# Loading the query weights as 64-partition halves of four and a half rows, and summing five full products per bank

## The chip, the cores and the metric

The kernel runs on one core of one Trainium2 chip. The metric is the device time of one execution in microseconds (us); lower is better. The time before is the median of three runs. One further execution was recorded by the hardware profiler, and the profile views come from that one.

## The reference

Two independent problems, A and B, have the same shapes: each is one decode step of attention with a sliding window over a key/value cache. All tensors are bf16.

```python
B, Sq, D = 2, 1, 576
Hq, Hkv, Sk, Dh = 32, 16, 16384, 128
W = 4096                                   # the last 4096 cached positions
q = (x @ wq)                               # [2, 1, 4096] -> 32 heads of 128
k = k_cache[:, :, Sk - W:, :]              # each of 16 kv heads serves 2 query heads
v = v_cache[:, :, Sk - W:, :]
p = softmax(q k^T * Dh ** -0.5)
o = p v
out = o.reshape(B, Sq, Hq * Dh) @ wo       # wo: [4096, 576]
# the outputs of A and B stand side by side: [2, 1, 1152]
```

Per problem wq is 576 x 4096 elements (4.72 MB), wo 4096 x 576 (4.72 MB), and the windows of k and v are 33.6 MB each; about 153 MB in all come from HBM.

## The kernel before

**Stream and ring.** A list, `stream`, sets the order of the large loads: wq of A, wq of B, then K slabs and V slabs in turn. A slab is [128 partitions, 16384 bf16], 32 KB per partition, and holds the whole window of 4 of the 32 pairs of batch and kv head: each of a pair's 32 partitions has 128 consecutive positions. The slabs go through a ring of `NR` = 4 slots; slab n uses slot n % 4 and waits, on the SP queue, for the last reader of slab n - 4 (`reader`). All large loads are issued in order from SP's one queue. `issue_wq` places the wq loads, `issue_slab` the K and V loads, `issue_wo` the loads of wo into `wob`.

**wq before.** A contraction row of wq is 4096 columns (8192 bytes), and there are 576 = 4 x 128 + 64 rows. The first 512 rows fill one ring slot, four consecutive rows per partition (32 KB). The last 64 rows are a separate transfer into `wqr`: each row is cut in two halves of 2048 columns, so that 128 partitions hold half a row (4 KB) each. `NFC` = 4 counts the full rows per partition.

**x and q.** x of A is loaded from the ACT queue, x of B from SP's behind the loads of A's wq. The transpose `f_xT` brings x to 128 partitions with five small matmuls against an identity: four for the full rows and one for a copy (`x_dup`) of the last 64 elements with each element doubled. ACT copies the result into `xT` (`f_xev`, L389); DVE multiplies the doubled part with a mask (`maskP`) of even and odd partitions (`f_xev2`, L397), so that each half row of `wqr` meets only its own x element. `do_qpair` (matmuls recorded at L450 and, for those that keep the weights, at L188) computes q for two groups of heads at a time into four PSUM banks of 512 columns: a bank sums four products from the ring slot and one from `wqr`. There are four such pairs, two per problem, 20 products of 512 columns each. `do_qrow` moves a finished q row to SBUF (ACT), transposes it in 32x32 blocks (DVE, L475) and keeps it in `qk` (ACT, L483); `do_zq` (POOL) spreads it into the zero-padded weights of the score product.

**Attention.** For each of 16 steps a K slab is transposed in four quarters by DVE into `xt` (`do_X`, L515; three buffers), multiplied with `zq` on PE into the score banks `ST` (`do_S`, L540), reduced and exponentiated (`do_max`, `do_nm`, `do_exp`), transposed back (`do_pC`), and multiplied with the V slab (`do_PV`, L631). The output projection (`do_proj`) follows per group with wo in `wob`.

**Memory shared over time.** `wob` holds 32 slots of wo; its second half is used early on, before wo arrives, for `wqr`, `qrow`, `qtr`, `xT`, `x_sb` and the identity (`early`). wo's first load waits for the last `qkeep`.

**Order.** Each engine runs its instructions in the order in which `S.add` recorded them, and waits on semaphores for what another engine or a DMA produces. All q pairs and q rows stand ahead of the first `do_X` on every engine.

Of the kernel before, what the change touches and what calls it, by code (L numbers as in the profile page):

```python
# [5 lines left out]
FP32 = mybir.dt.float32  # L6
# [53 lines left out]
def build_kernel(nc, probs, out, cfg=None):  # L60
# [24 lines left out]
    GPP = SPP // 2  # L85
    NFC = D // 128
    DREM = D - 128 * NFC
    assert DREM * 2 == 128 and NFC * HD == SLABW
    HH = HD // 2
    NXC = NFC + 2  # L90
    NOUT = wo0.shape[1]
# [22 lines left out]
    with es:  # L114
        sb = lambda name, shape, dt: es.enter_context(nc.sbuf_tensor(name, shape, dt))
        ring = sb("ring", [128, NR, SLABW], BF16)
        xt = sb("xt", [128, NKT, 2048], FP32)
        wob = sb("wob", [128, NSW, NOUT], BF16)
        used = [0]

        def early(shape):
            n = 1
            for d_ in shape:
                n *= d_
            a = wob[:, NSW // 2:NSW, :].rearrange("p s n -> p (s n)")[:, used[0]:used[0] + n]
            used[0] += n
            assert used[0] <= NSW // 2 * NOUT
            names = "abc"[:len(shape)]
            return a if len(shape) == 1 else a.rearrange("p (%s) -> p %s" % (" ".join(names), " ".join(names)), **dict(zip(names, shape)))
        wqr = early([NPROB, HH])  # L130
        qrow = early([1024])
        qtr = early([1024])
        xT = early([NXC, NPROB, 128])
        x_sb = early([D])[0:NPROB * Bb]
        x_dup = early([DREM, 2])[0:NPROB * Bb]
        ident_b = early([128])
# [18 lines left out]
        Rsb = [sb("Rsb%d" % n_, [128, Bb, n], BF16) for n_, n in enumerate((32, 16))]  # L155
        masks = sb("masks", [128, 30], BF16)
        maskS, mask16D, maskA, mask4S, maskJ, maskP = (masks[:, a_:b_] for a_, b_ in ((0, 8), (8, 16), (16, 20), (20, 24), (24, 28), (28, 30)))
        mask16S = sb("mask16S", [128, 16], BF16)
# [19 lines left out]
        ring_sem = [sem("ring%d" % r) for r in range(NR)]  # L178
        wq_sem = sem("wq")
        wo_sem = [sem("wo%d" % r) for r in range(2)]  # L180
# [21 lines left out]
        def load_x(P, eng):  # L202
# [5 lines left out]
        p_ident_b = S.add("pool", lambda e: e.affine_select(ident_b[:], ones_b[:], [[-1, 128]], ALU.is_equal, 0.0,  # L208
                                                           base=0, channel_multiplier=1), [p_ones_b], "ident_b")
        p_zxT = S.add("dve", lambda e: e.memset(xT[:].rearrange("c h p w -> c (h p w)").bitcast(FP32), 0.0), [], "zero_xT")  # L210
        p_zq = S.add("dve", lambda e: e.memset(zq[:].rearrange("d p z w -> d (p z w)").bitcast(FP32), 0.0), [], "zero_zq")
# [14 lines left out]
        for part, at in ((0, ("K", 5)), (1, ("V", 11)), (2, ("V", 12))):  # L226
            w_at.setdefault(at, []).append(part)

        slab_dma = {}
        pieces = []  # L230
# [8 lines left out]
        def issue_slab(n):  # L239
# [6 lines left out]
            src = src_t.rearrange("b h s d -> (b h) s d")[g::SPP, Sk - W:Sk, :].rearrange("c (r j) d -> r c (j d)", r=32)  # L246
            r = n % NR
            deps = [reader[n - NR]] if n >= NR else []
# [10 lines left out]
        def issue_wq(n, P):  # L259
            wqP = probs[P][3]  # L260
            r = n % NR
            deps = [reader[n - NR]] if n >= NR else []
            wq_dma[P] = dma_op("sp", wq_sem, 1, lambda e: e.dma_start(
                wqr[:, P, :], wqP[NFC * 128:D, :].rearrange("r (h n) -> r h n", h=2)).then_inc(wq_sem, 16), [], "wqr%d" % P)
            slab_dma[n] = dma_op("sp", ring_sem[r], 1, lambda e: e.dma_start(
                ring[:, r, :], wqP[0:NFC * 128, :].rearrange("(p s) n -> p (s n)", s=NFC)).then_inc(ring_sem[r], 16), deps, "wq%d" % P)

            if P == 0:
                for P_ in range(1, NPROB):
                    x_dma[P_] = load_x(P_, "sp")  # L270
# [96 lines left out]
        def f_xT(e, bank):  # L367
            last = None
            NB = NPROB * Bb
            for ch in range(NFC + 1):  # L370
                if ch < NFC:
                    src = x_sb[0:NB, 0:NFC * 128].rearrange("b (p s) -> b s p", s=NFC)[:, ch, :]
                else:
                    src = x_dup[0:NB, :, :].rearrange("b r t -> b (r t)")
                last = e.matmul(bank[:, ch * 4 * NB:(ch + 1) * 4 * NB], src, ident_b[0:NB, 0:NB].rearrange(  # L375
                    "k (p b) -> k p b", b=Bb).unsqueeze(2).broadcast_to([NB, NPROB, 4, Bb]), start=True, stop=True)
            return last
        issue_until(0)
        init_small()
        x_cd = S.add("dve", lambda e: e.tensor_copy(  # L380
            x_dup[:], x_sb[:, NFC * 128:D].unsqueeze(2).broadcast_to([NPROB * Bb, DREM, 2])), list(x_dma.values()), "xdup")
        init["maskP"] = S.add("dve", lambda e: e.tensor_reduce(
            maskP[:], ident_b[:].rearrange("d (r t) -> d t r", t=2), AX.X, ALU.max), [p_ident_b], "maskP")

        n_x, bank_x, op_xT = tb_job(f_xT, "xT", list(x_dma.values()) + [x_cd, p_ident_b])

        def f_xev(e):
            NB = NPROB * NFC * 4
            return e.activation(  # L389
                xT[:, 0:NFC].rearrange("c h p (a w) -> c (h p a) w", a=4)[:, :, 0:Bb],  # L390
                bank_x[:, 0:NB * Bb].rearrange("c (q b) -> c q b", b=Bb),
                ACTF.Copy)
        op_xev = S.add("act", f_xev, [op_xT, p_zxT], "xev")
        NB_ = NPROB * 4 * Bb

        def f_xev2(e):
            return e.tensor_tensor(  # L397
                xT[:, NFC:NXC].rearrange("c h p (a w) -> c h (p a) w", a=4)[:, :, :, 0:Bb],
                bank_x[:, NFC * NB_:(NFC + 1) * NB_].rearrange("c (q b) -> c q b", b=Bb).unsqueeze(1).broadcast_to([128, 2, NPROB * 4, Bb]),
                maskP[:].unsqueeze(2).unsqueeze(3).broadcast_to([128, 2, NPROB * 4, Bb]), ALU.mult)  # L400
        op_xev = S.add("dve", f_xev2, [op_xev, op_xT, init["maskP"]], "xev2")
        tb_consumer[n_x] = op_xev

# [20 lines left out]
        def do_qpair(i):  # L424
# [4 lines left out]
            banks = q_banks(i)  # L429
            mine = lambda ch: [b for b in range(4) if ch < NFC or b % 2 == ch - NFC]  # L430
            order = [NFC, NFC + 1] + list(range(NFC))
            if Gs[0] % GPP:
                order = order[::-1]
            todo_ = [(ch, b) for ch in order for b in mine(ch)]
            seen = {b: 0 for b in range(4)}
# [3 lines left out]
            for g in range(2):  # L439
                def fn(e, part=todo_[(0, ends[0])[g]:ends[g]]):  # L440
                    last = None
                    for ch, b in part:
                        c0 = (b % 2) * HH + 512 * (Gs[b // 2] % GPP)
                        w_ = ring[:, nq % NR, ch * HD + c0:ch * HD + c0 + 512] if ch < NFC else wqr[:, P, c0 - (b % 2) * HH:c0 - (b % 2) * HH + 512]
                        start, stop = seen[b] == 0, seen[b] == NFC
                        seen[b] += 1
                        if q_first[0] == (P, ch):
                            last = matmul_again(e, q_first[1], banks[b], w_, start, stop, False)
                        else:
                            last = q_first[1] = e.matmul(banks[b], xT[:, ch, P, :], w_, start=start, stop=stop)  # L450
                            q_first[0] = (P, ch)
                    return last
                before = [q_free.get((i - 1, b)) for b in range(4)] if g else []
                op = S.add("pe", fn, [slab_dma[nq], op_xev] + list(wq_dma.values()) + prev + before, "q%d" % Gs[g])
                reader[nq] = op
# [52 lines left out]
        def do_X(s, u):  # L508
# [3 lines left out]
            deps = [slab_dma[n]]  # L512
            if i >= NKT:
                deps.append(Sop[divmod(i - NKT, NU)])
            Xop[(s, u)] = S.add("dve", lambda e: e.transpose(  # L515
                xt[:, i % NKT, :].rearrange("k (j w) -> k j w", w=64),
                ring[:, n % NR, :].bitcast(FP32).rearrange("k (j q w) -> k q j w", q=4, w=64)[:, u]),
                deps, "X%d_%d" % (s, u))
# [99 lines left out]
        def do_PV(D_, rounds, wait):  # L618
# [7 lines left out]
            def f(e):  # L626
                last = None
                for jr in rounds:
                    for cb in range(4):
                        j0_ = JR * jr + 4 * cb  # L630
                        last = e.matmul(ACC[32 * cb:32 * cb + 32, 0:512],  # L631
                                        pC[:, D_ % NPT, j0_:j0_ + 4, :].rearrange("k j c -> k (j c)"),
                                        ring[:, n % NR, j0_ * 128:(j0_ + 4) * 128],
                                        start=(jr == 0), stop=(jr == last_r))
# [389 lines left out]
```

## Time and profile before

| quantity | value |
|---|---|
| median of 3 runs | 363.33 us (362.79 to 363.37) |
| the profiled execution | 363.02 us |
| its span in the profile | 361.8 us |
| mean granted TensorE clock | 0.882 |
| PE busy | 218.6 us (60%) |
| DVE busy | 200.9 us (56%) |
| ACT busy | 68.2 us (19%) |
| POOL busy | 35.3 us (10%) |
| read from HBM | 153.10 MB, 423 GB/s over the span |

The profiled execution is one execution; its span runs from the first to the last instruction, and 1.2 us of its time lie outside. A DMA's "time to landing" counts from its issue, so it includes the time for which the transfer stands in the queue behind others. A DMA share is the mean busy share of the core's 16 DMA engines.

### The profile page before, as it was taken

To read this page: it belongs to the slowest core of one execution; us is meant where nothing else is said; L and a number is where in the kernel's file an instruction comes from. 1 tells how busy PE (TensorE), PEld (TensorE's weight loads), DVE (VectorE), ACT (ScalarE), POOL (GpSimd) and SP (SyncE) were. 2 spreads that over 40 slices of the span, in tenths; PEclk is the share of its full clock that TensorE was granted. 3 is DMA by queue.
4 is the path that set the end of the run, shared out by engine and by line. 5 is a ranking of instruction groups with operands and counts; after the bars stand their busy time and mean duration, and the time that the engine had idled before them with its cause. 6 is when DMAs were issued, how large, how long until landed. Compare 5 with 4: busy or idle time off the path is not lost.

```text
span 361.8 us, 2730 instructions
## 1 busy us (share of the span) xinstructions
PE 218.6 (60%) x1318; PEld 55.8 (15%) x945; DVE 200.9 (56%) x175; ACT 68.2 (19%) x149; POOL 35.3 (10%) x55
## 2 busy tenths in 40 slices
PE   0399195763747207466574737766867707657786
PEld 0010021120111101112120201212121201211132
DVE  4112599846647019283756658392919239079931
ACT  1036502130203002103020203020201203002131
POOL 1000000004000400001300040002100040200020
PEclk9999689997889857969698978899898978969999
DMA  8999999999999999999999999999999999999996
GB/s 348 421 449 406 464 406 437 431 408 453 415 442 438 428 424 438 429 428 438 417 446 422 435 428 442 426 435 428 424 424 440 431 424 433 431 438 428 438 409 248
DMA packets 6491, 153.27 MB, mean 424 GB/s; under 512 B 712, under 2 KB 1232, under 8 KB 1616
## 3 DMA queue, kind: packets, MB, share of 16 engines
q1 hardware_dynamic: 6476, 153.10, 98.8%
q8 instruction: 9, 0.15, 0.2%
q14 instruction: 2, 0.02, 0.0%
q10 hardware_dynamic: 4, 0.00, 0.0%
HBM read 153.10 MB, written 0.00 MB: 423 GB/s over the span
## 4 chain that ended last, share of the span: by engine, by line
DMA 72%; DVE 17%; PE 7%; ACT 3%; SPq 1%; issue 0%
DMA ring<-in_B_k_cache_dram 34%; DMA ring<-in_A_k_cache_dram 27%; DVE xt L515 14%; DMA wob<-in_B_wo_dram 8%; DMA wob<-in_B_x_dram 3%; PE st L188 3%; PE st L540 3%; ACT wob L465 1%; DVE wob L475 1%; ACT qk L483 1%; PE st L450 1%; DVE m L550 1%; ACT wob L470 1%; DVE nM L563 0%; SPq L252 0%
## 5 line engine op out<-in xcount | busy, mean ns | idle before, releaser
L515 DVE STREAM_TRANSPOSE xt<-ring 128x2048 f32<-128x2048 f32 x64 | 145.3, 2284 | 86.6 <-DMA ring<-in_A_k_cache_dram 49.8
L540 PE MATMUL st<-xt,zq 128*128 128x512 bf16 x256 | 111.6, 436 | 122.6 <-DVE xt L515 98.1
L188 PE MATMUL st<-xt,zq 128*128 128x512 bf16 x256 | 110.1, 430 | 0.0
L540 PEld LDWEIGHTS st<-xt,zq 128*128 128x128 bf16 x256 | 27.1, 106 | 216.3 <-DVE xt L515 113.5
L631 PE MATMUL acc<-ring,pC 128*32 128x512 bf16 x512 | 32.5, 381 | 1.2 <-DMA ring<-in_B_v_cache_dram 1.2
L568 ACT ACTIVATE nMrep<-nM 1x128 f32<-1x128 f32 x16 | 4.9, 308 | 146.9 <-DVE nM L563 146.9
L643 ACT ACTIVATE acc_sb<-acc 128x512 bf16<-128x512 f32 x16 | 9.5, 596 | 79.9 <-PE acc L631 79.9
L593 DVE STREAM_TRANSPOSE pC<-pR 128x1024 bf16<-128x1024 bf16 x16 | 19.6, 1223 | 3.7 <-ACT pR L585 2.1
L650 POOL TENSOR_TENSOR acc_sb<-acc_sb,masks 128x1024 bf16<-128x1024 bf16 (+1 forms) x8 | 13.4, 1679 | 66.6 <-ACT acc_sb L643 66.6
L550 DVE TENSOR_REDUCE m<-st 128x1 f32<-128x1024 f32 x16 | 19.0, 1190 | 1.4 <-PE st L188 1.4
L502 POOL TENSOR_TENSOR zq<-qk,masks 128x128 bf16<-128x128 bf16 x16 | 6.3, 398 | 136.2 <-PE st L188 114.4
L585 ACT ACTIVATE pR<-st,bias_sb 128x1024 bf16<-128x1024 f32 x16 | 17.8, 1114 | 0.5
L475 DVE STREAM_TRANSPOSE wob<-wob 128x512 f32<-128x512 f32 x8 | 5.7, 711 | 20.3 <-ACT wob L465 12.9
L415 ACT ACTIVATE st<-maskB 128x1024 f32<-128x1024 bf16 x16 | 16.5, 1032 | 1.6 <-POOL rsel L600 0.4
L786 PE MATMUL ot<-wob,Rsb 128*2 128x512 bf16 x56 | 15.2, 390 | 0.0
L631 PEld LDWEIGHTS acc<-ring,pC 128*32 128x32 bf16 x512 | 12.4, 96 | 15.9 <-issue 3.2
L600 POOL TENSOR_TENSOR rsel<-masks,rsum 128x16 f32<-128x16 bf16 x8 | 1.7, 216 | 108.0 <-ACT pR L585 108.0
L188 PE MATMUL tb<-wob,Rsb 128*2 128x64 bf16 x56 | 10.9, 195 | 0.0
L375 PE MATMUL tb<-wob 4*128 4x16 bf16 x5 | 0.3, 179 | 14.5 <-DVE wob L380 14.5
L653 POOL TENSOR_TENSOR acc_sb<-acc_sb 128x512 bf16<-128x512 bf16 (+1 forms) x8 | 8.2, 1029 | 0.6
L188 PE MATMUL st<-ring,wob 128*128 128x512 bf16 x24 | 7.9, 445 | 0.0
L579 ACT ACTIVATE bias_sb<-tb 128x1 f32<-128x1 f32 x16 | 2.7, 171 | 24.8 <-PE tb L573 24.8
(89 smaller groups left out, 99.5 us busy)
## 6 DMA issues: line engine op xcount, KB each, us to landing
ring<-in_A_k_cache_dram SPq DMA_DIRECT2D x8, 4096.0 KB, 30.4
ring<-in_A_v_cache_dram SPq DMA_DIRECT2D x8, 4096.0 KB, 32.5
ring<-in_B_k_cache_dram SPq DMA_DIRECT2D x8, 4096.0 KB, 28.4
ring<-in_B_v_cache_dram SPq DMA_DIRECT2D x7, 4096.0 KB, 32.8
wob<-in_A_wo_dram SPq DMA_DIRECT2D x1, 4608.0 KB, 43.3
ring<-in_A_wq_dram SPq DMA_DIRECT2D x1, 4096.0 KB, 12.7
ring<-in_B_wq_dram SPq DMA_DIRECT2D x1, 4096.0 KB, 22.6
ring<-in_B_v_cache_dram SPq DMA_DIRECT2D x1, 3072.0 KB, 25.5
```

Source lines behind the costliest of these rows:

```text
L188: return e.add_instruction(mybir.InstMatmult(name=nc.get_next_instruction_name(), engine=i.engine, ins=[e.lower_ap(rhs), i.ins[1]], outs=[ ...
L415: chain[(s, "fill")] = S.add("act", lambda e: e.activation(ST[s % 2][:, :].rearrange("k (h j) -> k h j", h=2), maskB[:].unsqueeze(1).broad ...
L475: chain[(G, "qtr")] = S.add("dve", lambda e: e.transpose(qtr[:].bitcast(FP32), qrow[:].bitcast(FP32)), evs, "qtr%d" % G)
L515: Xop[(s, u)] = S.add("dve", lambda e: e.transpose(xt[:, i % NKT, :].rearrange("k (j w) -> k j w", w=64), ring[:, n % NR, :].bitcast(FP32) ...
L540: first = last = e.matmul(bank, zq[:, p4, s % NZQ, w0:w0 + 128], mv, start=False, stop=stop, skip_group_check=True)
L550: chain[(s, "max")] = S.add("dve", lambda e: e.tensor_reduce(m1[:, 0:1], ST[s % 2][:, :], AX.X, ALU.max), d, "max%d" % s)
L585: chain[(s, "exp")] = S.add("act", lambda e: e.activation(pR[:, :], ST[s % 2][:, :], ACTF.Exp, bias=bias_sb[:, 0:1], scale=SCALE, accum_ou ...
L593: chain[(s, "pC")] = S.add("dve", lambda e: e.transpose(pC[:, s % NPT, :, :].rearrange("k j c -> k (j c)"), pR[:, :]), d, "pC%d" % s)
L631: last = e.matmul(ACC[32 * cb:32 * cb + 32, 0:512], pC[:, D_ % NPT, j0_:j0_ + 4, :].rearrange("k j c -> k (j c)"), ring[:, n % NR, j0_ * 1 ...
L643: acc_ev[D_] = S.add("act", lambda e: e.activation(acc_sb[:, D_ % 2, :], ACC[:, :], ACTF.Copy), d, "accev%d" % D_)
L650: t = S.add("pool", lambda e: e.tensor_tensor(v, v, maskJ[:].unsqueeze(1).unsqueeze(3).broadcast_to([128, l1 - l0, 4, 128]), ALU.mult), [a ...
L786: first = e.matmul(OT[0:Bb, 0:NB0], l_, wob[:, w0 + s_, 0:NB0], start=start and begin, stop=end, skip_group_check=True)
```

## The change

All 576 rows of wq now come in one form. A problem's wq, read as one string of bytes, is cut into 128 pieces of 36,864 bytes, which is four and a half rows. Even pieces go to partitions 0 to 63 and odd pieces to partitions 64 to 127. An odd piece begins in the middle of a row, so it is written half a row (`HH` = 2048 columns) further on in its partition; this brings column c of every row to the same place in all partitions. Each half is one DMA of [64 partitions, 18432 bf16]; both stand on SP's queue where the two loads of wq stood.

A partition now spans five rows (`NFC` = 5, 40,960 bytes), of which half a row is filled with zeros by DVE (`f_zw`, four memsets): the last half row on partitions 0 to 63, the first on 64 to 127. Because this is 8192 bytes more than a ring slot, `ring`, `xt` and `wob` become parts of one tensor `big`: A's wq ends with slot 0 and starts in the last `xt` buffer, B's wq fills slot 3 and runs into the start of `wob`. The slots are used in the order 0, 3, 1, 2. The third X transpose, the first to write that `xt` buffer, waits for the last product that reads A's wq.

x is gathered by two ACT copies into `x_s`, five columns for the even and five for the odd partitions; five small matmuls transpose them, and one ACT copy fills `xT`. `x_dup`, `maskP`, `f_xev2` and `wqr` go. Each bank of q sums five products of 512 columns with all 128 partitions; there are 20 products per pair, as before.

```diff
-    NFC = D // 128
+    NFC = D // 128 + 1
...
+        big = sb("big", [128, WOB0 + NSW * NOUT], BF16)
+        xt = big[:, 0:RING0].bitcast(FP32).rearrange("k (n w) -> k n w", n=NKT)
+        ring = big[:, RING0:WOB0].rearrange("k (n w) -> k n w", n=NR)
+        wob = big[:, WOB0:WOB0 + NSW * NOUT].rearrange("k (s n) -> k s n", n=NOUT)
+        wq_at = [RING0 - EXT, WOB0 - SLABW]
...
+        def f_zw(e):
+            last = None
+            for a_ in wq_at:
+                for e_ in range(2):
+                    z0 = a_ + (1 - e_) * (NFC * HD - HH)
+                    last = e.memset(big[64 * e_:64 * e_ + 64, z0:z0 + HH].bitcast(FP32), 0.0)
+            return last
+        p_zw = S.add("dve", f_zw, [], "zero_w")
...
+        slot = [(0, 3, 1, 2)[n % NR] for n in range(len(stream))]
...
-            wq_dma[P] = dma_op("sp", wq_sem, 1, lambda e: e.dma_start(
-                wqr[:, P, :], wqP[NFC * 128:D, :].rearrange("r (h n) -> r h n", h=2)).then_inc(wq_sem, 16), [], "wqr%d" % P)
-            slab_dma[n] = dma_op("sp", ring_sem[r], 1, lambda e: e.dma_start(
-                ring[:, r, :], wqP[0:NFC * 128, :].rearrange("(p s) n -> p (s n)", s=NFC)).then_inc(ring_sem[r], 16), deps, "wq%d" % P)
+            w = wqP.rearrange("r n -> (r n)").rearrange("(k e n) -> e k n", e=2, k=64)
+            NW = D * HD // 128
+            wq_dma[P] = [dma_op("sp", wq_sem[P], 1, lambda e, e_=e_: e.dma_start(
+                big[64 * e_:64 * e_ + 64, wq_at[P] + HH * e_:wq_at[P] + HH * e_ + NW], w[e_]).then_inc(wq_sem[P], 16), [], "wq%d_%d" % (P, e_))
+                for e_ in range(2)]
...
-        x_cd = S.add("dve", lambda e: e.tensor_copy(
-            x_dup[:], x_sb[:, NFC * 128:D].unsqueeze(2).broadcast_to([NPROB * Bb, DREM, 2])), list(x_dma.values()), "xdup")
+        x_cd = S.add("act", lambda e: e.activation(x_s[:, :, 0:64], x_sb[:, 0:D].rearrange("b (k s) -> b s k", k=64)[:, 0:NFC, :], ACTF.Copy),
+                     list(x_dma.values()), "xs0")
+        x_cd = S.add("act", lambda e: e.activation(x_s[:, :, 64:128], x_sb[:, 0:D].rearrange("b (k s) -> b s k", k=64)[:, NFC - 1:2 * NFC - 1, :], ACTF.Copy),
+                     [x_cd], "xs1")
...
-        op_xev = S.add("dve", f_xev2, [op_xev, op_xT, init["maskP"]], "xev2")
...
-            mine = lambda ch: [b for b in range(4) if ch < NFC or b % 2 == ch - NFC]
-            order = [NFC, NFC + 1] + list(range(NFC))
+            order = list(range(NFC))
...
-                op = S.add("pe", fn, [slab_dma[nq], op_xev] + list(wq_dma.values()) + prev + before, "q%d" % Gs[g])
+                op = S.add("pe", fn, wq_dma[P] + [op_xev, p_zw] + prev + before, "q%d" % Gs[g])
...
-            if i >= NKT:
-                deps.append(Sop[divmod(i - NKT, NU)])
+            deps.append(Sop[divmod(i - NKT, NU)] if i >= NKT else reader[pos[("Q", 0)]])
```

More of the change, by code (lines that the diff above doesn't have):

```diff
@@ L85, in build_kernel @@
     GPP = SPP // 2
-    NFC = D // 128
-    DREM = D - 128 * NFC
-    assert DREM * 2 == 128 and NFC * HD == SLABW
+    NFC = D // 128 + 1
     HH = HD // 2
-    NXC = NFC + 2
+    EXT = NFC * HD - SLABW
+    assert 2 * D == 128 * (2 * NFC - 1) and 0 < EXT <= 4096
     NOUT = wo0.shape[1]
@@ L115, in build_kernel @@
         sb = lambda name, shape, dt: es.enter_context(nc.sbuf_tensor(name, shape, dt))
[L116 to L119, printed above, removed]
+        RING0 = NKT * 4096
+        WOB0 = RING0 + NR * SLABW
+        big = sb("big", [128, WOB0 + NSW * NOUT], BF16)
[3 more added lines that the diff above has]
+        wq_at = [RING0 - EXT, WOB0 - SLABW]
+        used = [EXT]
         def early(shape):
@@ L124, in early @@
                 n *= d_
-            a = wob[:, NSW // 2:NSW, :].rearrange("p s n -> p (s n)")[:, used[0]:used[0] + n]
+            a = big[:, WOB0 + used[0]:WOB0 + used[0] + n]
             used[0] += n
-            assert used[0] <= NSW // 2 * NOUT
+            assert used[0] <= NSW * NOUT
             names = "abc"[:len(shape)]
             return a if len(shape) == 1 else a.rearrange("p (%s) -> p %s" % (" ".join(names), " ".join(names)), **dict(zip(names, shape)))
-        wqr = early([NPROB, HH])
         qrow = early([1024])
         qtr = early([1024])
-        xT = early([NXC, NPROB, 128])
+        xT = early([NFC, NPROB, 128])
         x_sb = early([D])[0:NPROB * Bb]
-        x_dup = early([DREM, 2])[0:NPROB * Bb]
+        x_s = early([NFC, 128])[0:NPROB * Bb]
         ident_b = early([128])
@@ L155, in build_kernel @@
         Rsb = [sb("Rsb%d" % n_, [128, Bb, n], BF16) for n_, n in enumerate((32, 16))]
-        masks = sb("masks", [128, 30], BF16)
-        maskS, mask16D, maskA, mask4S, maskJ, maskP = (masks[:, a_:b_] for a_, b_ in ((0, 8), (8, 16), (16, 20), (20, 24), (24, 28), (28, 30)))
+        masks = sb("masks", [128, 28], BF16)
+        maskS, mask16D, maskA, mask4S, maskJ = (masks[:, a_:b_] for a_, b_ in ((0, 8), (8, 16), (16, 20), (20, 24), (24, 28)))
         mask16S = sb("mask16S", [128, 16], BF16)
@@ L178, in build_kernel @@
         ring_sem = [sem("ring%d" % r) for r in range(NR)]
-        wq_sem = sem("wq")
+        wq_sem = [sem("wq%d" % n_) for n_ in range(2)]
         wo_sem = [sem("wo%d" % r) for r in range(2)]
@@ L246, in issue_slab @@
             src = src_t.rearrange("b h s d -> (b h) s d")[g::SPP, Sk - W:Sk, :].rearrange("c (r j) d -> r c (j d)", r=32)
-            r = n % NR
+            r = slot[n]
             deps = [reader[n - NR]] if n >= NR else []
@@ L260, in issue_wq @@
             wqP = probs[P][3]
-            r = n % NR
-            deps = [reader[n - NR]] if n >= NR else []
-            wq_dma[P] = dma_op("sp", wq_sem, 1, lambda e: e.dma_start(
-                wqr[:, P, :], wqP[NFC * 128:D, :].rearrange("r (h n) -> r h n", h=2)).then_inc(wq_sem, 16), [], "wqr%d" % P)
-            slab_dma[n] = dma_op("sp", ring_sem[r], 1, lambda e: e.dma_start(
-                ring[:, r, :], wqP[0:NFC * 128, :].rearrange("(p s) n -> p (s n)", s=NFC)).then_inc(ring_sem[r], 16), deps, "wq%d" % P)
+            w = wqP.rearrange("r n -> (r n)").rearrange("(k e n) -> e k n", e=2, k=64)
[3 more added lines that the diff above has]
+                for e_ in range(2)]
             if P == 0:
@@ L369, in f_xT @@
             NB = NPROB * Bb
[L370 to L375, printed above, removed]
+            for ch in range(NFC):
+                last = e.matmul(bank[:, ch * 4 * NB:(ch + 1) * 4 * NB], x_s[:, ch, :], ident_b[0:NB, 0:NB].rearrange(
                     "k (p b) -> k p b", b=Bb).unsqueeze(2).broadcast_to([NB, NPROB, 4, Bb]), start=True, stop=True)
@@ L379, in build_kernel @@
         init_small()
-        x_cd = S.add("dve", lambda e: e.tensor_copy(
-            x_dup[:], x_sb[:, NFC * 128:D].unsqueeze(2).broadcast_to([NPROB * Bb, DREM, 2])), list(x_dma.values()), "xdup")
-        init["maskP"] = S.add("dve", lambda e: e.tensor_reduce(
-            maskP[:], ident_b[:].rearrange("d (r t) -> d t r", t=2), AX.X, ALU.max), [p_ident_b], "maskP")
-        n_x, bank_x, op_xT = tb_job(f_xT, "xT", list(x_dma.values()) + [x_cd, p_ident_b])
+        x_cd = S.add("act", lambda e: e.activation(x_s[:, :, 0:64], x_sb[:, 0:D].rearrange("b (k s) -> b s k", k=64)[:, 0:NFC, :], ACTF.Copy),
+                     list(x_dma.values()), "xs0")
+        x_cd = S.add("act", lambda e: e.activation(x_s[:, :, 64:128], x_sb[:, 0:D].rearrange("b (k s) -> b s k", k=64)[:, NFC - 1:2 * NFC - 1, :], ACTF.Copy),
+                     [x_cd], "xs1")
+        n_x, bank_x, op_xT = tb_job(f_xT, "xT", [x_cd, p_ident_b])
         def f_xev(e):
@@ L389, in f_xev @@
             return e.activation(
-                xT[:, 0:NFC].rearrange("c h p (a w) -> c (h p a) w", a=4)[:, :, 0:Bb],
+                xT[:].rearrange("c h p (a w) -> c (h p a) w", a=4)[:, :, 0:Bb],
                 bank_x[:, 0:NB * Bb].rearrange("c (q b) -> c q b", b=Bb),
@@ L393, in build_kernel @@
         op_xev = S.add("act", f_xev, [op_xT, p_zxT], "xev")
[L394 to L400, printed above, removed]
-        op_xev = S.add("dve", f_xev2, [op_xev, op_xT, init["maskP"]], "xev2")
         tb_consumer[n_x] = op_xev
@@ L429, in do_qpair @@
             banks = q_banks(i)
-            mine = lambda ch: [b for b in range(4) if ch < NFC or b % 2 == ch - NFC]
-            order = [NFC, NFC + 1] + list(range(NFC))
+            order = list(range(NFC))
             if Gs[0] % GPP:
                 order = order[::-1]
-            todo_ = [(ch, b) for ch in order for b in mine(ch)]
+            todo_ = [(ch, b) for ch in order for b in range(4)]
             seen = {b: 0 for b in range(4)}
@@ L442, in fn @@
                     for ch, b in part:
-                        c0 = (b % 2) * HH + 512 * (Gs[b // 2] % GPP)
-                        w_ = ring[:, nq % NR, ch * HD + c0:ch * HD + c0 + 512] if ch < NFC else wqr[:, P, c0 - (b % 2) * HH:c0 - (b % 2) * HH + 512]
-                        start, stop = seen[b] == 0, seen[b] == NFC
+                        c0 = wq_at[P] + ch * HD + (b % 2) * HH + 512 * (Gs[b // 2] % GPP)
+                        w_ = big[:, c0:c0 + 512]
+                        start, stop = seen[b] == 0, seen[b] == NFC - 1
                         seen[b] += 1
@@ L512, in do_X @@
             deps = [slab_dma[n]]
-            if i >= NKT:
-                deps.append(Sop[divmod(i - NKT, NU)])
+            deps.append(Sop[divmod(i - NKT, NU)] if i >= NKT else reader[pos[("Q", 0)]])
             Xop[(s, u)] = S.add("dve", lambda e: e.transpose(
                 xt[:, i % NKT, :].rearrange("k (j w) -> k j w", w=64),
-                ring[:, n % NR, :].bitcast(FP32).rearrange("k (j q w) -> k q j w", q=4, w=64)[:, u]),
+                ring[:, slot[n], :].bitcast(FP32).rearrange("k (j q w) -> k q j w", q=4, w=64)[:, u]),
                 deps, "X%d_%d" % (s, u))
@@ L632, in f @@
                                         pC[:, D_ % NPT, j0_:j0_ + 4, :].rearrange("k j c -> k (j c)"),
-                                        ring[:, n % NR, j0_ * 128:(j0_ + 4) * 128],
+                                        ring[:, slot[n], j0_ * 128:(j0_ + 4) * 128],
                                         start=(jr == 0), stop=(jr == last_r))
```

## The prediction

> **What bounds the kernel now.** I read the page first: the slices, the DMA queues and the chain.
>
> ```profile
> DMA  8999999999999999999999999999999999999996
> GB/s 348 421 449 406 464 406 437 431 408 453 415 442 438 428 424 438 429 428 438 417 446 422 435 428 442 426 435 428 424 424 440 431 424 433 431 438 428 438 409 248
> DMA packets 6491, 153.27 MB, mean 424 GB/s; under 512 B 712, under 2 KB 1232, under 8 KB 1616
> ...
> q1 hardware_dynamic: 6476, 153.10, 98.8%
> ...
> DMA 72%; DVE 17%; PE 7%; ACT 3%; SPq 1%; issue 0%
> ```
>
> Every slice but the first and last has the 16 DMA engines over 90% busy, and one queue, SP's, uses 98.8% of them. No compute engine is above 60%. The kernel ends when 153 MB have been read, so a microsecond added to the queue's transfers is a microsecond of the result unless the queue had been dry, and it never is. The small packets tell how a transfer is divided: the 44 bulk transfers and four two-row ones (two x, two output) of the issue list give 712 packets under 512 B, just 44 x 16 + 4 x 2. I read that as one completion mark per engine used: 128 rows go to 16 engines, two rows to two. By the same division 64 rows go to 16 engines, four rows each.
>
> Second, the stages (columns: stage, length, busy time of five engines, clock, DMA share, GB/s).
>
> ```profile
> 0.00:5.00 5.00, 0.00 (x0) 0.00 (x0) 3.62 (x13) 1.28 (x1) 0.99 (x7) 1.00 0.79 302
> 5.00:15.00 10.00, 0.32 (x5) 0.23 (x5) 0.41 (x2) 0.17 (x1) 0.00 (x0) 1.00 1.00 426
> 15.00:25.00 10.00, 9.58 (x32) 1.10 (x9) 1.52 (x4) 2.02 (x7) 0.28 (x1) 1.00 0.97 419
> ...
> 65.00:300.00 235.00, 137.51 (x851) 36.81 (x629) 133.62 (x101) 37.72 (x69) 27.85 (x36) 0.86 1.00 431
> ```
>
> wq occupies the first 25 us, at 419 to 426 GB/s once started; the steady stage runs at 431. Third, the issue list (last column: us to landing) and the timeline of the opening.
>
> ```profile
> ring<-in_A_k_cache_dram SPq DMA_DIRECT2D x8, 4096.0 KB, 30.4
> ...
> ring<-in_A_wq_dram SPq DMA_DIRECT2D x1, 4096.0 KB, 12.7
> ring<-in_B_wq_dram SPq DMA_DIRECT2D x1, 4096.0 KB, 22.6
> ```
>
> ```profile
> 1.02 0.70 DVE L210 MEMSET wob<- 128x768 f32 x1 [1.02 <-PEq L1009]
> ...
> 14.20 0.21 DVE L380 COPY wob<-wob 4x128 bf16<-4x128 bf16 x1 [9.47 <-DMA wob<-in_B_x_dram]
> 14.83 0.22 ACT L389 ACTIVATE wob<-tb 128x64 bf16<-128x64 f32 x1 [12.19 <-PE tb L375]
> 15.42 0.59 PE L450 MATMUL st<-wob 128*128 128x512 bf16 x1 [0.63 <-DVE wob L397]
> 26.99 0.54 SPq L256 DMA_DIRECT2D ring<-in_A_v_cache_dram  x1
> 36.04 0.54 SPq L256 DMA_DIRECT2D ring<-in_A_k_cache_dram  x1
> 41.79 11.04 DVE L515 STREAM_TRANSPOSE xt<-ring 128x2048 f32<-128x2048 f32 x5
> ```
>
> A slab of 4.19 MB needs 4.19 / 0.431 = 9.7 us of the queue but lands 30 us after its issue: two others are queued ahead. wq A lands at 1.25 + 12.7 = 13.95 us, wq B at 2.45 + 22.6 = 25.05 (issued at 1.25 and 2.45 on SP's timeline), K0 and K1 behind them at about 34.7 and 44.4. The q products start at 15.42, 1.2 us after x B has come.
>
> **The DMA term.** Bytes are unchanged: per problem 576 x 8192 B = 4.72 MB, 9.44 MB in both. At 431 GB/s that is 21.9 us of the queue. The change replaces two transfers per problem that fill all 128 partitions (4 KB pieces and 32 KB slab) by two that fill 64 each, one after the other in the same queue. Its cost has two bounds. If the limit sits in the engines (431 / 16 = 26.9 GB/s each), 16 engines with four rows each still give 431 and the cost is 0. If it sits where data enters the partitions, half the partitions take half: 215 GB/s, 43.8 us, +21.9 us. The trace does not separate the two, since every large transfer in it fills 128 partitions with all 16 engines. I take the second: the only rate any row shows is 431 / 128 = 3.37 GB/s into a partition, the same in the wq stage and in the steady one, and keeping 431 would need 6.7, which nothing here has reached. The second half can't use the idle partitions beside the first, because all engines work through the first transfer's packets before the second's. [...]
>
> Going the other way, 256 packets of 4 KB disappear in favour of 36,864 B rows (wo A already has such rows, inside the 431 stage). If all of the slowness of the 15 to 25 us stage were theirs, they would be worth 9.44/0.419 - 9.44/0.431 = 0.6 us; that stage is mostly 32 KB packets, so I take 0.2 us of gain.
>
> **Issues and waits on SP.** Five DMAs stand ahead of K0 before and after, in the same places, at 0.31 to 0.50 us each: nothing. Nothing new waits on SP. The ring is as deep as before: V0 still waits for the last product of wq A, K2 for that of wq B. With the forecast rate wq A lands at 13.95 + 10.95 = 24.9, x B behind it, products from 26.4; V0's issue moves from 26.99 to about 38. wq B lands at 25.05 + 21.9 = 46.9; from the start of its products to K2's issue was 26.6 to 36.04, 9.4 us, so K2 is issued near 56.4. The queue holds K0 and K1 until 44.4 + 21.9 = 66.3 and V0 until 76, so V0 has 28 us and K2 some 20 us to spare: the queue stays full, and what is late next is everything behind wq by the same 21.9 us. Nothing later gives it back, since share 1.00 from 65 to 300 us leaves no hole to fill.
>
> **The compute terms.** Four memsets of 1024 words on DVE: 0.70 us for 768 gives 0.93 each, 3.7 us; removed is a sixth of the xT memset (0.1). They end the early DVE work near 8.4 instead of 4.7 us (4.37 + 0.35), before x B at 14.2: hidden; without that cover they cost at most 3.7. The identity on POOL waits behind them for ones_f, but is first read by the maximum's transpose, far later. On the way from x B to the first product, DVE's copy (0.21) and product (0.19) go, and two ACT copies come. Four partitions by 320 elements is between the 0.22 of L389 and the 0.58 of a 512-element copy on ACT, so 0.4 to 1.1 us for two, I take 0.5: the q products start about 0.1 later (bounds 0 to 0.7), hidden by V0's 28 us (or 17 us at the old rate: K1 lands at 44.4). PE: 80 products of 512 columns before and after, four to a bank's fifth replaced one for one. New wait: the third X transpose uses the buffer in which wq A ends, so it waits for wq A's last product; behind it on DVE are all later transposes. But DVE's program has all eight q-row transposes ahead of X, and X began at 41.79, 15 us after that product: nothing.
>
> **Sum.** The profiled run took 363.02 us (span 361.8), the median is 363.33, 0.3 above. From the median: 363.33 + 21.9 - 0.2 = 385.0 us.
>
> **Rivals.** *The engines are the limit, not the partitions* (place: the wq stage; it decides if that stage keeps over 98% of 431). For it: the engine share is 1.00 everywhere, which is also what a limited engine looks like. Against it: the doubled rate per partition. Then nothing but the 4 KB packets counts: 363.33 - 0.2 = 363.1, at best 362.7. *The two halves overlap*: 8 of 16 engines get ahead and fill the odd half while the rest finish the even one. Then only the first transfer goes at half rate, 2.36/0.431 = 5.5 us: 368.6; with overlap half of the time 374. The engines start together and share the same load, which speaks against it. *The start is helped*: the first 5 us moved 302 GB/s, a hole of 5 x (1 - 302/431) = 1.5 us; were the 4 KB packets to blame for half of it, 362.4. But the queue starts with issue and latency whatever the packets are. *A drain between halves*: if each of the three later transfers started as emptily as the first, 3 x 1.5 = 4.5 more, 389.5; slabs that follow each other without a hole speak against it.
>
> **How the numbers follow.** Half rate 0.78 (383.5 to 387; to 389 with drains), overlap 0.08, engines the limit 0.11, start helped 0.03. About 0.2% (0.73 us) is what a measurement of this kernel can tell from no change. Slower is the first two, 0.86; of the engine case 0.09 is within 0.2% and 0.02 faster, so same 0.09 and faster 0.05. The range runs from 374, half overlap, to 389: 0.78 and half of the overlap case make 0.82.
>
> **What would show it.** Right: 210 to 220 GB/s with the engines still 90% busy (packets twice as long) until about 45 us, wq A at 25 and wq B at 47 us, V0 issued near 38, X from about 62, 431 GB/s from there on. Wrong: over 400 GB/s in 5 to 25 us (engine limit); 215 for the first 5 us only and 400 after (overlap); a dry queue before 76 us (a late product). A span below 370 refutes the half rate.

## The result, and the profile after

The changed kernel takes 386.62 us (median of 5 runs, 386.35 to 386.85) against 362.81 us before (median of 5): a ratio of 1.065 with a 95% interval of 1.0634 to 1.0665, 23.8 us slower. The forecast was 385.0. The profiled execution's span is 385.3 us, 23.5 above the 361.8 of before; the time of it is 386.62.

The page of the changed kernel, slices and queue:

```profile
GB/s 184 218 211 199 219 422 429 432 420 436 429 429 434 435 428 436 432 435 423 435 432 432 427 432 425 435 427 435 435 429 427 432 420 444 430 432 429 435 416 248
DMA packets 6235, 153.27 MB, mean 398 GB/s; under 512 B 712, under 2 KB 1232, under 8 KB 1360
...
q1 hardware_dynamic: 6220, 153.10, 98.7%
```

The first five slices, 48 us, run at about half of the others; from the sixth on it is the old kernel. The 256 packets of 4 KB are gone (1616 under 8 KB became 1360), the 712 smallest are unchanged, so by the prediction's reading of these marks the 64-row loads do use 16 engines each. The stages of the changed kernel (columns as before: five engines, clock, DMA share, GB/s):

```profile
5.00:15.00 10.00, 0.00 (x0) 0.00 (x0) 4.62 (x16) 0.00 (x0) 0.29 (x1) 1.00 0.97 203
15.00:25.00 10.00, 0.00 (x0) 0.00 (x0) 0.00 (x0) 0.00 (x0) 0.00 (x0) 1.00 1.02 210
25.00:35.00 10.00, 6.98 (x28) 0.81 (x10) 0.00 (x0) 2.65 (x4) 0.00 (x0) 1.00 0.98 203
...
65.00:300.00 235.00, 142.93 (x837) 37.28 (x618) 143.71 (x104) 37.13 (x71) 24.19 (x32) 0.84 1.00 431
```

The DMA share is 0.97 to 1.02 at 203 to 210 GB/s, and 1.00 at 431 later: the engines count as busy in both and move half in the first. So the share near 1 is no sign here that the engines are the limit. The chain of waits and the opening of the timeline:

```profile
3.09 45.93 DMA big<-in_B_wq_dram
```

```profile
25.96 0.78 ACT L386 ACTIVATE big<-big 4x320 bf16<-4x320 bf16 x1 [23.31 <-DMA big<-in_B_x_dram]
26.77 0.78 ACT L388 ACTIVATE big<-big 4x320 bf16<-4x320 bf16 x1
...
28.32 0.59 PE L446 MATMUL st<-big 128*128 128x512 bf16 x1 [0.42 <-ACT big L394]
...
38.88 0.54 SPq L267 DMA_DIRECT2D big<-in_A_v_cache_dram  x1
...
49.07 0.61 PE L446 MATMUL st<-big 128*128 128x512 bf16 x1 [10.22 <-DMA big<-in_B_wq_dram]
...
59.69 0.54 SPq L267 DMA_DIRECT2D big<-in_A_k_cache_dram  x1
...
65.22 6.66 DVE L510 STREAM_TRANSPOSE big<-big 128x2048 f32<-128x2048 f32 x3
```

wq B lands at 3.09 + 45.93 = 49.0 us instead of 25.05, 24 us later, and the end moves by 23.5. V0 is issued at 38.88 and K2 at 59.69, while the queue still holds K0 and K1 until about 49.0 + 2 x 9.7 = 68.4 us and V0 until 78: the queue never ran dry. The loss is all in the wq stage.

### The profile page after: what moved, and what is told of

It reads as the page before. It is cut to its first block, busy times and chain, and to the rows that moved or that the text cites. A ratio compares the mean times of both kernels' runs of the same rounds, so it can differ in the third digit from the quotient of the medians.

```text
span 385.3 us, 2728 instructions
## 1 busy us (share of the span) xinstructions
PE 222.3 (58%) x1316; PEld 56.1 (15%) x941; DVE 203.9 (53%) x176; ACT 69.9 (18%) x151; POOL 35.3 (9%) x55
## 2 busy tenths in 40 slices
DMA packets 6235, 153.27 MB, mean 398 GB/s; under 512 B 712, under 2 KB 1232, under 8 KB 1360
## 4 chain that ended last, share of the span: by engine, by line
DMA 76%; DVE 14%; PE 9%; SPq 1%; issue 0%
DMA big<-in_B_k_cache_dram 31%; DMA big<-in_A_k_cache_dram 25%; DVE big L510 13%; DMA big<-in_B_wq_dram 12%; DMA big<-in_B_wo_dram 7%; PE st L190 4%; PE st L535 3%; DVE nM L558 0%; SPq L274 0%; PE tb L190 0%; PE tb L548 0%; PE st L446 0%; PE ot L190 0%; SPq L263 0%; DVE m L545 0%
## 5 line engine op out<-in xcount | busy, mean ns | idle before, releaser
L510 DVE STREAM_TRANSPOSE big<-big 128x2048 f32<-128x2048 f32 x64 | 145.3, 2284 | 85.7 <-DMA big<-in_A_k_cache_dram 49.9
L535 PE MATMUL st<-big,zq 128*128 128x512 bf16 x256 | 114.1, 446 | 119.4 <-DVE big L510 94.9
L190 PE MATMUL st<-big,zq 128*128 128x512 bf16 x256 | 112.0, 438 | 0.0
L535 PEld LDWEIGHTS st<-big,zq 128*128 128x128 bf16 x256 | 27.5, 107 | 216.1 <-DVE big L510 110.1
L626 PE MATMUL acc<-big,pC 128*32 128x512 bf16 x512 | 32.5, 381 | 1.0 <-DMA big<-in_B_v_cache_dram 1.0
L471 DVE STREAM_TRANSPOSE big<-big 128x512 f32<-128x512 f32 x8 | 5.7, 712 | 49.7 <-ACT big L461 42.4
L781 PE MATMUL ot<-big,Rsb 128*2 128x512 bf16 x56 | 14.9, 385 | 0.0
L626 PEld LDWEIGHTS acc<-big,pC 128*32 128x32 bf16 x512 | 12.7, 96 | 15.3 <-issue 3.2
L190 PE MATMUL tb<-big,Rsb 128*2 128x64 bf16 x56 | 10.9, 194 | 0.0
L190 PE MATMUL st<-big 128*128 128x512 bf16 x30 | 10.7, 478 | 0.2 <-issue 0.2
L446 PE MATMUL st<-big 128*128 128x512 bf16 x9 | 4.2, 466 | 10.6 <-DMA big<-in_B_wq_dram 10.2
## 6 DMA issues: line engine op xcount, KB each, us to landing
big<-in_A_wq_dram SPq DMA_DIRECT2D x2, 2304.0 KB, 19.7
big<-in_B_v_cache_dram SPq DMA_DIRECT2D x1, 3072.0 KB, 25.6
```

The source lines that it names most:

```text
L190: return e.add_instruction(mybir.InstMatmult(name=nc.get_next_instruction_name(), engine=i.engine, ins=[e.lower_ap(rhs), i.ins[1]], outs=[ ...
L510: Xop[(s, u)] = S.add("dve", lambda e: e.transpose(xt[:, i % NKT, :].rearrange("k (j w) -> k j w", w=64), ring[:, slot[n], :].bitcast(FP32 ...
L535: first = last = e.matmul(bank, zq[:, p4, s % NZQ, w0:w0 + 128], mv, start=False, stop=stop, skip_group_check=True)
L626: last = e.matmul(ACC[32 * cb:32 * cb + 32, 0:512], pC[:, D_ % NPT, j0_:j0_ + 4, :].rearrange("k j c -> k (j c)"), ring[:, slot[n], j0_ * ...
L781: first = e.matmul(OT[0:Bb, 0:NB0], l_, wob[:, w0 + s_, 0:NB0], start=start and begin, stop=end, skip_group_check=True)
```

## The experiments

Theory 1 supposes that partitions share the places where data enters them ("entries"), and that the rate goes by how many of these a transfer reaches; on the way it parts into 1a, how many it reaches in all, and 1b, how many its engines write at one moment, which the author took to mean half rate, 384 us, for e5's alternate partitions. Theory 2, the wording of the prediction: each partition takes at most about 3.3 GB/s. Theory 3: the pair of transfers costs by itself. Theory 4: the four-and-a-half-row pieces or the new compute cost. Entries are the author's supposition: no run shows them, their number, which partitions share one, or which engine moves which row. What the runs show is the rate and the time for each choice of partitions. In e1 to e5 only the 32 KB slab load of the kernel before is cut differently:

```diff
-            slab_dma[n] = dma_op("sp", ring_sem[r], 1, lambda e: e.dma_start(
-                ring[:, r, :], wqP[0:NFC * 128, :].rearrange("(p s) n -> p (s n)", s=NFC)).then_inc(ring_sem[r], 16), deps, "wq%d" % P)
+            wsrc = wqP[0:NFC * 128, :].rearrange("(p s) n -> p (s n)", s=NFC)
...
+            def f_cut(e):
+                last = None
+                for p_, c_ in cuts:
+                    last = e.dma_start(ring[p_, r, c_], wsrc[p_, c_]).then_inc(ring_sem[r], 16)
+                return last
+            slab_dma[n] = dma_op("sp", ring_sem[r], len(cuts), f_cut, deps, "wq%d" % P)
```

Runs without an interval are single runs; all effects read from them are over 10 us, unless the text says otherwise.

**e1: two transfers of 128 partitions, half the columns each.**

> The kernel before, with only the 32 KB slab load of each wq issued as two transfers, each over all 128 partitions and half of the columns (16 KB per partition). Bytes, partitions and products as before. Theory 1, shared entries (what counts is how many of the partitions' entries the 16 engines write at one moment): 362.8, within 0.7. Theory 2, a fixed 3.3 GB/s per partition (the prediction's wording): 362.8, within 0.7. Theory 3, the cost comes from issuing wq as a pair of transfers one behind the other, whatever they fill: up to the 23.5 us that the changed kernel lost, about 384.

Measured 362.97 us against 362.92, ratio 1.0002 (0.9993 to 1.0012). Two loads in place of one, each over all 128 partitions, cost nothing; theory 3 falls.

**e2: two transfers of 64 partitions, 0 to 63 and 64 to 127.**

> The kernel before, with only the slab load of each wq issued as two transfers, partitions 0 to 63 and 64 to 127, 32 KB rows. The 4 KB pieces, the x path, the products and the zeros stay as before. Theories 1 and 2: 2 x 4.19 MB at the 205 GB/s of the changed kernel's wq stage take 40.9 us instead of 19.5 at 431, +21.4: 384. Theory 4, the cost lies in the four-and-a-half-row pieces (their odd starts in HBM, the packets of 36,864 B) or in the new compute ahead of q: 363.

Measured 385.56 us, +22.6. The kernel before, with its own pieces and compute, shows the loss as soon as its slab is cut by partitions. Its stage from 5 to 15 us:

```profile
5.00:15.00 10.00, 0.00 (x0) 0.00 (x0) 0.00 (x0) 0.00 (x0) 0.00 (x0) 1.00 1.01 210
```

**e3: four transfers of 32 partitions.**

> The kernel before, with only the slab load of each wq issued as four transfers of 32 partitions each. Theory 1, with partitions 0 to 31 and 32 to 63 behind the same entries: 32 partitions go as fast as 64, 205 GB/s, +21.4: 384. Theory 2, a fixed rate per partition: 102 GB/s, 8.39 MB take 82 us, +62: 425. [...] Theory 3 (cost per transfer in the queue): twice the loss of two halves, about 405.

Measured 383.57 us, +20.7. Its stage from 5 to 15 us:

```profile
5.00:15.00 10.00, 0.00 (x0) 0.00 (x0) 0.00 (x0) 0.00 (x0) 0.00 (x0) 1.00 1.01 210
```

32 partitions take 210 GB/s, as many as 64 do: 6.6 GB/s for each, twice the 3.3 that theory 2 allows. The transfers did not run side by side: the landing marks of A's four (16 to a transfer, one per engine by the prediction's reading) end at 9.6, 14.5, 19.7 and 24.5 us, 1.05 MB every 5 us. The prediction's per-partition limit is wrong.

**e4: partitions 32 to 95, then 0 to 31, then 96 to 127.**

> The kernel before, with only the slab load of each wq issued as three transfers: partitions 32 to 95, 0 to 31, 96 to 127. [...] Half of 8.39 MB at 205: 20.5 instead of 9.7 us, +10.7: 373.5. Theory 2, a fixed rate per partition: middle +10.7, outer two at 102 GB/s +31.2, together +42: 405. A theory by which 64 rows are always half rate, and 32 rows too: 384.

Measured 388.54 us: all three expectations missed (373.5 by theory 1, with the middle at 431 GB/s and the rest at 205; 405; 384), and it is slower than e2 (385.56). The page gives 14.0 us from issue to landing for the middle load of A and 32.2 for that of B (the time of the slab's 16th landing mark), so a whole-rate middle did not come out of the kernel as a gain. From its page:

```profile
DMA  9999999999999999999999999999999999999991
GB/s 288 179 288 183 251 413 433 433 425 430 432 433 428 429 429 435 430 427 432 430 427 433 432 430 433 433 432 433 433 423 434 428 431 436 432 433 430 422 391 61
```

The landing marks are out of step here. Ten of A's slab come between 9.4 and 10.4 us and the next only at 14.4; in e6 all 16 marks of A's middle come between 10.3 and 11.1. In e4 they stay apart: the marks of K0 spread over 7 us (0.8 in e6), and the last slice of the run moves 61 GB/s (248 before), so part of the loss is a tail at the end. Why they come apart is not shown; e6 keeps the cuts and changes the order.

**e5: even partitions, then odd partitions.**

> The kernel before, with only the slab load of each wq issued as two transfers, the even partitions (0, 2, ... 126) and the odd ones. Theory 1a, a transfer's rate goes by how many entries its partitions reach in all: every other partition reaches all of them, 362.9. [...] Theory 2, fixed rate per partition: 384.

Measured 364.29 us, +1.3 (a single run, but 0.9 above the highest of the 15 runs of before). Its stages:

```profile
0.00:5.00 5.00, 0.00 (x0) 0.00 (x0) 3.62 (x13) 1.28 (x1) 0.99 (x7) 1.00 0.72 250
5.00:10.00 5.00, 0.00 (x0) 0.00 (x0) 0.00 (x0) 0.00 (x0) 0.00 (x0) 1.00 0.89 360
10.00:15.00 5.00, 0.00 (x0) 0.00 (x0) 0.26 (x2) 0.00 (x0) 0.00 (x0) 1.00 0.99 423
```

64 partitions per transfer, and no half rate: A's two loads landed 4.9 us apart (10.9 and 15.8 us), 2.1 MB at 429 GB/s. That is theory 1a, but for the 1.3 us; theory 2 and half rate throughout (1b) fall. The rate climbs from 360 GB/s between 5 and 10 us to 423 between 10 and 15. What makes it climb, and whether that is the 1.3 us, is not shown.

**e6: the middles of A and B first, the outer rows after.**

```diff
...
+            if P == 0:
+                for P_ in range(NPROB):
+                    wqr_load(P_)
+                for P_ in range(NPROB):
+                    rows(P_, P_, [slice(32, 96)])
+            slab_dma[n] = rows(n, P, [slice(0, 32), slice(96, 128)])
```

> The kernel before with the wq loads in another order: the 4 KB pieces of A and B, then partitions 32 to 95 of both slabs (A, B), then partitions 0 to 31 and 96 to 127 of A, x of B, and the same two of B. Theory 1b: the middle transfers have one engine per entry, 4.19 MB at 431 GB/s in 9.7 us, so both have landed by about 15 us; the outer ones have two engines per entry, 4.19 MB at 205 in 20.5 us. +10.7 in all: 373.6. [...] Theory 2 or any rule that 64 rows are half rate: the second middle lands at about 24 us, and 384 or more.

Measured 374.14 us, where 373.6 was expected. The stages and the landings (last column):

```profile
5.00:10.00 5.00, 0.00 (x0) 0.00 (x0) 0.00 (x0) 0.00 (x0) 0.00 (x0) 1.00 0.97 383
10.00:15.00 5.00, 0.00 (x0) 0.00 (x0) 0.00 (x0) 0.00 (x0) 0.00 (x0) 1.00 1.03 426
15.00:20.00 5.00, 0.00 (x0) 0.00 (x0) 0.00 (x0) 0.00 (x0) 0.00 (x0) 1.00 1.12 242
20.00:25.00 5.00, 0.00 (x0) 0.00 (x0) 0.00 (x0) 0.00 (x0) 0.00 (x0) 1.00 1.00 210
```

```profile
ring<-in_A_wq_dram SPq DMA_DIRECT2D x1, 2048.0 KB, 9.4
ring<-in_B_wq_dram SPq DMA_DIRECT2D x1, 2048.0 KB, 14.2
ring<-in_A_wq_dram SPq DMA_DIRECT2D x2, 1024.0 KB, 20.7
```

Same kernel, same queue: partitions 32 to 95 arrive at 426 GB/s, 0 to 31 and 96 to 127 at 210. The middle of B lands 4.8 + (2.37 - 1.71) = 5.5 us after that of A, 2.1 MB at 383. So it is neither the number of partitions nor a rate for each that counts, but which ones: 64 partitions half below and half above 64 load at about the whole rate (383 to 426 GB/s), those on one side at half (210, in e2 and here). Against e4, the order of the same cuts is worth 14.4 us, with both 4 KB loads put first as well; what makes the order count is not shown.

**e7: the changed kernel, odd pieces issued from ACT's queue.**

```diff
-            wq_dma[P] = [dma_op("sp", wq_sem[P], 1, lambda e, e_=e_: e.dma_start(
+            wq_dma[P] = [dma_op(("sp", "act")[e_], wq_sem[P], 1, lambda e, e_=e_: e.dma_start(
...
-        issue_until(0)
+        issue_until(1)
```

> The changed kernel with the odd pieces (partitions 64 to 127) issued from ACT's queue and the even ones from SP's, both at the start. Theory 1b with an engine that serves one packet at a time and all engines in step: still two engines per entry, 386. If an engine works on both queues at once, both halves' entries are busy and the rate is whole: 363 to 365. [...]

Measured 388.04 us. With one half on each of two queues the stage is no faster. Its stages, and the landings of A's halves (last column):

```profile
15.00:20.00 5.00, 0.00 (x0) 0.00 (x0) 0.00 (x0) 0.00 (x0) 0.00 (x0) 1.00 1.11 236
20.00:25.00 5.00, 0.00 (x0) 0.00 (x0) 0.00 (x0) 0.00 (x0) 0.00 (x0) 1.00 1.09 236
25.00:30.00 5.00, 0.30 (x5) 0.20 (x5) 0.00 (x0) 1.79 (x3) 0.00 (x0) 1.00 1.04 221
30.00:35.00 5.00, 3.76 (x9) 0.41 (x3) 0.00 (x0) 0.00 (x0) 0.00 (x0) 1.00 0.71 155
```

```profile
big<-in_A_wq_dram SPq DMA_DIRECT2D x1, 2304.0 KB, 21.9
big<-in_A_wq_dram ACTq DMA_DIRECT2D x1, 2304.0 KB, 29.8
```

A window counts a packet where it starts, hence 236 and 155; the mean of the four is 212. Both queues were served together: the first half of A took 21.9 us to land, where it took 14.3 in the changed kernel with nothing beside it. A second queue did not raise the rate; why not, with both halves in flight, is not shown.

**e8: one transfer of 128 partitions by 36,864 bytes.**

```diff
...
-            w = wqP.rearrange("r n -> (r n)").rearrange("(k e n) -> e k n", e=2, k=64)
...
+            w = wqP.rearrange("r n -> (r n)").rearrange("(p n) -> p n", p=128)
-            wq_dma[P] = [dma_op("sp", wq_sem[P], 1, lambda e, e_=e_: e.dma_start(
-                big[64 * e_:64 * e_ + 64, wq_at[P] + HH * e_:wq_at[P] + HH * e_ + NW], w[e_]).then_inc(wq_sem[P], 16), [], "wq%d_%d" % (P, e_))
-                for e_ in range(2)]
+            wq_dma[P] = [dma_op("sp", wq_sem[P], 1, lambda e: e.dma_start(
+                big[:, wq_at[P]:wq_at[P] + NW], w).then_inc(wq_sem[P], 16), [], "wq%d" % P)]
```

> The changed kernel with wq of a problem as one transfer of 128 partitions by 36,864 bytes, the odd pieces not shifted by half a row, and the upper half row zeroed on all partitions by one memset. The products are the same in number and shape but take the odd pieces' columns at the wrong place, so q is not the reference's; this kernel is for its time. Theories 1 and 2: the four-and-a-half-row form costs nothing, 363.33 - 0.2 by the prediction's working, so within 0.7 of the kernel before, if anything 0.1 to 0.3 below. Theory 4 (the odd row starts, the packets of 36,864 B or the new compute ahead of q cost the time): 386.

Measured 363.10 us against 362.95, ratio 1.0008 (0.9999 to 1.0017). The landings:

```profile
big<-in_A_wq_dram SPq DMA_DIRECT2D x1, 4608.0 KB, 13.6
big<-in_B_wq_dram SPq DMA_DIRECT2D x1, 4608.0 KB, 23.6
```

Odd starts in HBM, 36,864 B rows, two more ACT copies and five full products per bank cost nothing that can be seen; theory 4 falls. Neither do they gain: the interval reaches from 0.04 us below the kernel before to 0.6 above.

**e9 and e10: the change on alternate partitions, and the control for its order.**

```diff
...
-                big[64 * e_:64 * e_ + 64, wq_at[P] + HH * e_:wq_at[P] + HH * e_ + NW], w[e_]).then_inc(wq_sem[P], 16), [], "wq%d_%d" % (P, e_))
+                big[e_:128:2, wq_at[P] + HH * e_:wq_at[P] + HH * e_ + NW], w[e_]).then_inc(wq_sem[P], 16), [p_zw[P]], "wq%d_%d" % (P, e_))
...
+            if nxt[0] == 0:
+                issue_slab(pos[("K", 0)])
...
```

> The changed kernel with even pieces on the even partitions and odd pieces on the odd ones (a load to every other partition), both half-row strips zeroed on all partitions ahead of the loads, and K0's slab issued first so that the queue works while the strips are zeroed. The output is the reference's. Theory 1 in the form that run e5 left (a transfer that reaches all entries ends up at the whole rate after some microseconds of sorting out): the 23.5 us go but for the 1.3 that the alternate slabs lost, 364.3, between 363.3 and 365.5. If the half rate belongs to 64-row transfers of four and a half rows in another way: 386.

> The kernel before with K0's slab issued ahead of wq, nothing else changed: the control for the order in e9. The queue is full in either order and the q products have slack, so 362.9 within 0.7. If the later start of q (about 25 us instead of 15) starves the ring, up to some microseconds more.

e9: 364.98 us against 362.87, ratio 1.0065 (1.004 to 1.0089). The whole change, with the pieces laid on every other partition, the zeros ahead of the loads and K0 first, loses 2.1 us instead of 23.8. Its wq stage runs at the whole rate:

```profile
15.00:20.00 5.00, 0.00 (x0) 0.00 (x0) 0.00 (x0) 0.00 (x0) 0.00 (x0) 1.00 1.10 472
20.00:25.00 5.00, 0.00 (x0) 0.00 (x0) 0.00 (x0) 0.69 (x1) 0.00 (x0) 1.00 0.91 391
25.00:30.00 5.00, 3.62 (x13) 0.61 (x8) 0.00 (x0) 1.11 (x3) 0.00 (x0) 1.00 1.01 435
```

This profiled execution took 366.87 us, more than the other five; behind wq, from 55 to 65 us, it moves 393 GB/s, where e10 moves 423.

e10: 363.92 us, ratio 1.0045 (1.0024 to 1.0067), outside the expected 0.7: by the medians, 1.05 of e9's 2.1 us belong to the order, though the two intervals overlap. Why K0 ahead of wq costs 1.05 us is open. In e10's trace the first 5 us move 210 GB/s, as in e9's, where the kernel before moved 302; that is 0.46 MB, about 1.1 us of the queue, and fits, but no run isolates it.

No version is faster than the kernel before: the form with the fewest transfers (e8, whose q is not the reference's) is level with it, so no run shows anything for this change to win here.

## Why the prediction was right

- *The bound* (the SP queue; a microsecond in it is one in the result): right. wq B lands 24.0 us later, the span grows by 23.5, and the rate from 65 to 300 us is 431 GB/s in both.
- *The DMA term*: right in direction, place and size (+21.9 forecast), somewhat too small. The forecast halved 431 to 215; the stage shows 203, 210 and 203, mean 205. A window counts a packet where it starts; by the landing marks of wq A (26.4 us) and wq B (49.0), 4.72 MB took 22.6 us, 209 GB/s. So 9.44 MB take 45.2 to 46.0 us, not 43.8. The result lies 1.6 us above the forecast: from the 362.81 us measured beside it, the 21.9 and these 1.4 to 2.2 give 386.1 to 386.9; 386.62 was measured. Why the rate is 3 to 5% below half of 431 is open.
- *The reason given for it* (a limit per partition, 3.37 GB/s) was wrong, and that the number came out all the same is luck of this cut. e3 moved 6.6 GB/s into each of 32 partitions. For halves by partition number theories 1 and 2 both give half; for the cuts of e3, e5 and e6 they part, and a rate for each partition fails in all three (383.57 us for 425, 364.29 for 384, 374.14 for 384 or more). In these runs the rate went by which partitions a load reaches; why it does is not shown, and e4 met neither forecast.
- *The gain of 0.2 us from the 4 KB packets*: not there (e8).
- *The waits*: right. wq A was forecast to land at 25 and landed at 26.4, V0 was forecast at 38 and issued at 38.88, K2 at 56.4 and 59.69, X at 62 and 65.22, the late ones late by wq B's extra 2 us and one more. The first product was forecast at 26.4 and ran at 28.32: x B landed about 0.8 us later than the forecast allows, and the two ACT copies took 0.78 us each where 0.5 was taken for both. With V0 not due before 68.4 us it cost nothing. The early DVE work was forecast to end near 8.4 us and ended at 9.9, still long before x B. The wait for the last product of A's wq, which the code gives to each of the first three X transposes, cost nothing: that product ended before 39 us and X began at 65.22.
- *Rivals*: that the engines are the limit is refuted by e2 and e3 (half the rate at engine share 1.01). Overlap of the halves did not happen in the changed kernel (203 to 210 GB/s throughout; A's halves landed one behind the other, at 15.1 and 26.4 us), and two queues, which served both halves together, gained nothing (e7, 388.04 us). A drain between halves shows neither in e1, where pairs of transfers cost nothing, nor as a dip in the stage. The start is not helped: without the 4 KB packets e8 moves 236 GB/s in the first 5 us, the kernel before 302.

## What to carry to other kernels

Before cutting a load by partitions, ask which partitions each piece covers: pieces that stay below or above partition 64 run at about half rate here (210 GB/s in e2, e3 and e6), pieces that reach both sides, or every other partition, at nearly the whole (360 to 423 in e5, 383 to 426 in e6, 391 to 472 in e9). Mixing the two kinds load by load, as e4 does, lost 25.6 us, more than halves throughout (e2, 22.6). A busy share near 1 for the DMA engines went with 210 GB/s (e2, 1.01) as with 431 (before, 1.00): read GB/s beside it, stage by stage. When data must differ by partition (here, the half-row shift), a layout in which the difference falls on alternate partitions kept nearly the whole rate (e9, 364.98 us for the 362.87 of before).

## What the runs showed of the hardware that was not expected

- 32 partitions (e3, 210 GB/s) load as fast as 64 on one side of partition 64 (e2, 210), and partitions 32 to 95 (e6, 426 GB/s) twice as fast as either.
- Alternate partitions (e5) start slower (360 GB/s from 5 to 10 us) and reach 423 from 10 to 15.
- The order of loads of different shape matters: e4 and e6 move the same rows by the same cuts, and differ by 14.4 us (388.54 and 374.14, single runs; in e6 the 4 KB loads come first as well). In e4 the 16 landing marks of K0 spread over 7 us (0.8 in e6), and the last slice of the run moves 61 GB/s (248 before).
